# A fused attention and feed-forward kernel: shorter k transposes, a moved fill mark, a split last tile, and more zero matmuls at the start

## The chip, the cores and the metric

The kernel runs on one core of a Trainium2 chip. A core has a matrix engine (TensorE, "PE" in the profile; its weight loads are listed as "PEld"), a vector engine (VectorE, "DVE"), a scalar engine (ScalarE, "ACT"), a general engine (GpSimd, "POOL") and SyncE ("SP"), which here only issues transfers. Transfers are carried by 16 DMA engines that all queues share. The metric is the device time of one execution in microseconds (us); several runs are made, and their median is used.

## The reference

Attention over 8 batches and 8 heads, with 16 extra "beacon" keys and values put ahead of the 576 ordinary ones, and causal masking of the ordinary ones. The output, 4608 rows of 512, goes through a multiplicative feed-forward network:

```python
k_all = np.concatenate([beacon_k, k], axis=2)      # 16 + 576 keys per head, head size 64
v_all = np.concatenate([beacon_v, v], axis=2)
scores = 1/sqrt(64) * q @ k_all^T, masked, softmax
x = (softmax @ v_all) as (4608, 512)
out = (((x @ w1) * (x @ w2)) @ w3) @ w_out         # w1, w2: 512 x 1024; w3: 1024 x 1024; w_out: 1024 x 512
```

Inputs and output are float32.

## The kernel before

Arithmetic is in 16-bit floats with 32-bit accumulation. w3 and w_out are multiplied into one matrix `Wt` (1024 x 512) first, so that the network needs two products per 512 rows of x: `ff_ab` (x times w1 and w2, their product in `gT`) and `ff_out` (`gT` times `Wt`). The 4608 rows make nine chunks, numbered 0 to 8. A chunk is 96 units, and a unit is one 512-column matmul: 64 units of `ff_ab`, 32 of `ff_out` (four output tiles, `mt` 0 to 3, of eight matmuls each).

Attention goes in 64 steps, eight per batch: for each of four pairs of heads an even and an odd step. `scores(s)` makes the score groups of a step (two groups each; the last group of an odd step is ten matmuls with 80 query columns, which need all five key tiles), `exps` their exponentials on ACT, `mask` the masking on DVE, `values(s)` the products with v and the normalization into `x16`.

There are three stages.

1. Up to step 15 (batches 0 and 1) the instructions stand in an order written out by hand, `ORDER` (L40). Each word is one small piece: `cR` and `cW` cast parts of w3 and w_out, `W` transposes a row tile of w3 on TensorE (L341), `w` evacuates it, `M` multiplies two 128-row pieces into an accumulator of `Wt` (L357, "fuse"), `o` reorders loaded q or k (L185), `T` transposes it on TensorE, `S`, `E`, `K`, `V`, `N` are scores, exponentials, masks, value sums and normalizations. `Z.3` is three matmuls with zeros (L239, 432 columns each); ten of them come ahead of the whole order. `G` puts the later loads on POOL's queue.
2. From step 16 on a loop (L678) emits for each step the next step's scores, this step's values and, between them, `fill[s]` units of the feed-forward network. `fill` comes from `marks` (L532): pairs of a step and the number of units that are to be out when this step begins, with even spacing in between. Units count from 40 at step 16; chunk n begins at unit 32 + 96 (n - 1), so chunk 4 at 320.
3. After step 63 what is left of the network follows without a break (L702).

q, k and v of each batch are loaded by POOL in 128-row chunks, cast on the way (L128, L137, L141 for the beacons). For batches 2 to 7, q and k are then transposed by DMA from SP's queue: `transpose_qk` (L149) for chunks 0 to 4, five of q and five of k. The last q chunk has 64 rows. The last k chunk has 80 (576 + 16 - 512), but its transpose takes all 128; the 48 pad rows of `k16s` were set to zero at the start (L317), and the columns that they would fill in `kTs` too (L249). Batches 0 and 1 are transposed on TensorE instead. Two sets of buffers alternate between batches. When the last pair of heads of a batch is normalized, five DMA transposes on SP bring `x16` into `xT` (L520). So SP's queue is, in order: the q and k transposes of a batch, the x transposes of the batch before, those of the next batch, and so on. POOL's queue holds, in the order of emission, the loads of v for the next batch, of q and k for the batch after that, and the stores of output tiles (L413) of all chunks but the last two; those of the last two go on SP's. At most eight of a queue's transfers are outstanding at a time: the next waits for the eighth before it to land.

## Time and profile before

| | |
|---|---|
| median of 5 runs | 301.95 us (301.19 to 302.72) |
| the profiled execution | 301.76 us |
| its span, first to last instruction | 299.7 us |
| PE, PEld, DVE, ACT, POOL busy, share of the span | 96%, 50%, 55%, 53%, 44% |
| 512-column matmul of `ff_ab` and `ff_out`, x864 | 379 ns each, from issue to end; back to back one each 0.216 us |
| copy of 512 columns from the accumulator, ACT L379 and DVE L411 | 597 and 692 ns |
| DMA transposes of q and k, issue to landing, median | 8.9 us |

How to read it: the span is cut into 40 slices of 7.5 us; a digit is the busy share of an engine in a slice, in tenths. "PEclk" is the clock that was granted to TensorE. A row of stretches (they are given with their start and end) lists for each engine how long it was busy and, in brackets, with how many instructions, then the granted clock, the DMA share and GB/s. A timeline row is start, duration, engine, line, operation, output and input, and in square brackets the idle time before it and what ended that. A row of waits is who waited for whom: us in total, times, longest. A row of the chain of waits is start, duration, and what was done or waited for.

### The profile page before, as it was taken

How to read it: one execution, taken by the hardware profiler on the slowest of the kernel's cores; microseconds unless marked ns; L12 is line 12 of the kernel's file. 1: busy time of each engine (PE TensorE's matmuls, PEld its weight loads, DVE VectorE, ACT ScalarE, POOL GpSimd, SP SyncE). 2: the span in 40 equal slices, each digit the busy share in tenths (PEclk: the TensorE clock that was granted, in tenths of full speed). 3: DMA queues.
4: the chain of work that ended last, by engine and by line, in shares of the span. 5: the costliest groups of instructions: out<-in, count | busy, mean ns of one | idle time of the engine just before them, and what ended most of it. 6: DMA issues, size and time to landing. Idle time of an engine off the chain costs nothing.

```text
span 299.7 us, 6953 instructions
## 1 busy us (share of the span) xinstructions
PE 287.4 (96%) x2801; PEld 150.3 (50%) x2801; DVE 164.1 (55%) x386; ACT 160.3 (53%) x226; POOL 131.4 (44%) x183
## 2 busy tenths in 40 slices
PE   6698999999999999999999999999999999999994
PEld 2445766564455555545554555455555544444441
DVE  3337867774556665465555555555556554344342
ACT  3638868672587756645663667466644650320310
POOL 5679968844756735462565327735311002000000
PEclk9599999999999999999999999999999999999999
DMA  7999999999999999999999999999991015103003
GB/s 255 351 165 180 154 184 190 149 131 130 153 221 143 141 128 164 128 155 187 151 141 127 139 211 115 155 139 247 144 236 72 0 35 148 42 0 140 0 31 112
DMA packets 160256, 42.67 MB, mean 142 GB/s; under 512 B 152288, under 2 KB 155872, under 8 KB 160224
## 3 DMA queue, kind: packets, MB, share of 16 engines
q0 software_dynamic: 112032, 24.91, 97.8%
q1 hardware_dynamic: 48192, 17.31, 40.5%
q8 instruction: 22, 0.36, 0.5%
q14 instruction: 10, 0.08, 0.1%
HBM read 39.32 MB, written 9.44 MB: 163 GB/s over the span
## 4 chain that ended last, share of the span: by engine, by line
PE 74%; DMA 15%; issue 2%; POOL 2%; SPq 2%; DVE 2%; ACT 1%; POOLq 0%; DVEq 0%
PE pm L367 32%; PE pm L401 17%; PE pv L491 9%; PE ps L448 8%; DMA qT<-q 5%; DMA k<-in_k_dram 5%; DMA kT<-k 3%; PE ps L357 3%; PE pm L357 3%; DMA gT<-in_moe_w_dram 2%; PE pm L341 1%; POOL q L128 1%; PE pm L217 1%; POOL k L137 1%; SPq L153 1%
## 5 line engine op out<-in xcount | busy, mean ns | idle before, releaser
L367 PE MATMUL pm<-xT,w 128*128 128x512 f16 x576 | 133.1, 379 | 0.0
L463 ACT ACTIVATE pT<-ps 128x736 f16<-128x736 f32 (+3 forms) x128 | 104.9, 864 | 51.7 <-PE ps L448 48.7
L367 PEld LDWEIGHTS <-w 128*128 128x128 f16 x576 | 53.0, 98 | 57.5 <-issue 0.4
L379 ACT ACTIVATE a_sb<-pm 128x512 f32<-128x512 f32 x70 | 41.8, 597 | 60.4 <-PE pm L367 59.6
L381 DVE TENSOR_TENSOR gT<-pm,a_sb 128x512 f16<-128x512 f32 x72 | 49.6, 690 | 37.9 <-PE pm L367 35.2
L401 PE MATMUL pm<-Wt,gT 128*128 128x512 f16 x288 | 65.6, 379 | 0.4 <-DVE gT L381 0.4
L137 POOL DMA_DIRECT2D va<-in_v_dram x40 | 34.0, 858 | 23.4 <-DMA k<-in_k_dram 11.4
L401 PEld LDWEIGHTS <-gT 128*128 128x128 f16 x288 | 27.2, 98 | 31.1 <-issue 0.5
L491 PE MATMUL pv<-va,pT 128*128 128x65 f16 x960 | 40.8, 194 | 0.7 <-DVE pT L475 0.7
L491 PEld LDWEIGHTS <-pT 128*128 128x128 f16 x960 | 33.7, 97 | 10.6 <-issue 5.2
L413 POOL DMA_DIRECT2D out_dram<-ot x28 | 15.5, 556 | 52.8 <-DVE ot L411 36.7
L411 DVE TENSOR_SCALAR ot<-pm 128x512 f32<-128x512 f32 x36 | 24.9, 691 | 24.9 <-PE pm L401 24.8
L508 DVE RECIPROCAL rd<-pv 128x4 f32<-128x4 f32 x64 | 12.1, 189 | 47.7 <-PE pv L491 47.5
L448 PE MATMUL ps<-qT,kT 64*128 64x80 f16 (+3 forms) x704 | 35.1, 228 | 1.7 <-ACT Wt L591 0.7
L128 POOL DMA_DIRECT2D q<-in_q_dram x35 | 30.0, 858 | 13.5 <-DMA va<-in_v_dram 6.3
L137 POOL DMA_DIRECT2D k<-in_k_dram x35 | 29.7, 848 | 11.5 <-DMA va<-in_v_dram 9.4
L448 PEld LDWEIGHTS <-kT 64*128 64x128 f16 x704 | 20.6, 95 | 26.9 <-issue 23.9
L509 DVE TENSOR_TENSOR x<-pv,rd 128x256 f16<-128x256 f32 x64 | 31.4, 491 | 2.4
L475 DVE TENSOR_TENSOR pT<-pT,MB 128x512 f16<-128x512 f16 (+1 forms) x64 | 20.4, 325 | 0.5 <-ACT pT L463 0.2
L475 DVE TENSOR_TENSOR pT<-pT,MA 128x480 f16<-128x480 f16 x32 | 12.8, 399 | 0.4 <-ACT pT L463 0.4
L341 PE MATMUL pm<-ident,xT 128*128 128x128 f16 x64 | 6.3, 260 | 3.6 <-DVE q L170 3.6
L357 PE MATMUL ps<-wo,wT 128*128 128x512 f16 x32 | 9.2, 438 | 0.0
(70 smaller groups left out, 111.6 us busy)
## 6 DMA issues: line engine op xcount, KB each, us to landing
out_dram<-ot POOLq DMA_DIRECT2D x28, 256.0 KB, 8.9
q<-in_q_dram POOLq DMA_DIRECT2D x28, 128.0 KB, 9.9
va<-in_v_dram POOLq DMA_DIRECT2D x24, 128.0 KB, 9.3
k<-in_k_dram POOLq DMA_DIRECT2D x21, 128.0 KB, 9.9
w<-in_moe_w_dram POOLq DMA_DIRECT2D x4, 512.0 KB, 8.7
out_dram<-ot SPq DMA_DIRECT2D x8, 256.0 KB, 2.0
gT<-in_moe_w_dram SPq DMA_DIRECT2D x3, 512.0 KB, 5.9
gT<-in_moe_w_out_dram SPq DMA_DIRECT2D x2, 512.0 KB, 6.1
```

The costliest lines, as they stand in the source:

```text
L128: nc.gpsimd.dma_start(q16s[b % NB2][:rows, c, :].rearrange("s (h d) -> s h d", h=H), q[b, :, ds(c * P, rows), :].rearrange("h s d -> s h d"),)
L137: nc.gpsimd.dma_start(dst[ds(p0, rows)], src[b, :, ds(s0, rows), :].rearrange("h s d -> s h d"))
L357: nc.tensor.matmul(acc, wT[:, rt, :], wo16[:, rt, :], start=(rt == 0), stop=(rt == NFT - 1),)
L367: nc.tensor.matmul(pm, w12[:, kt, ds(i * DF + kf * P, P)], xT[:, kt, ds(mc * 512, 512)], start=(kt == 0), stop=(kt == NKT - 1),)
L379: nc.scalar.activation(a_sb, pm, AF.Copy, scale=GS)
L381: nc.vector.tensor_tensor(gT[:, kf, :], pm, a_sb, ALU.mult)
L401: nc.tensor.matmul(pm, gT[:, kf, ts(mt, P)], Wt[:, kf, :], start=(kf == 0), stop=(kf == NFT - 1),)
L448: nc.tensor.matmul(ps[:, hh, ds(col, n)], kT[ds(hh * 64, 64), t, ts(jt, P)], qT[ds(hh * 64, 64), t, ds(q0, n)],)
L463: nc.scalar.activation(pT[:, :, ds(GO[g], GW[g])], pss[s, j][:, :, 0 : GW[g]], AF.Exp, scale=scale)
L475: nc.vector.tensor_tensor(blk, blk, m.unsqueeze(1).to_broadcast([P, 2, n]), ALU.mult)
L491: nc.tensor.matmul(pv[:, 2 * n + hh, 0:65], pT[:, hh, ds(col, P)], va[:, jt, 2 * t + hh, 0:65], start=(jn == 0), stop=(jn == len(BLK[i]) - 1),
L509: nc.vector.tensor_tensor(x16[:, ds(tiles[0], ni), ds(t * P, P)].rearrange("p i (h d) -> p i h d", h=2), pv[:, 0 : 2 * ni, 0:64].rearrange ...
```

## The change

Four places, the arithmetic being the same:

- `ORDER`: `Z.3` becomes `Z.7`, four more matmuls with zeros ahead of `W.3`, the second w3 tile to be transposed.
- `transpose_qk`: the last chunk of k is transposed with its 80 rows instead of 128.
- `ff_out`: the last output tile (chunk 8, `mt` 3) is computed, evacuated and stored in two halves of 256 columns. The first is evacuated by DVE, the second by ACT. All other tiles are as before.
- `marks`: a point (43, 320) comes in between (32, 200) and (58, 516). Before, the straight line between these two passed 320 units within step 41.

```diff
 ORDER = """
-cW.0.0.A cR.1.D cW.0.1.A cR.3.D cR.0.A W.1 w.1.A G cR.2.D Z.3 W.3 w.3.A cW.1.1.A W.0
+cW.0.0.A cR.1.D cW.0.1.A cR.3.D cR.0.A W.1 w.1.A G cR.2.D Z.7 W.3 w.3.A cW.1.1.A W.0
...
         rows = min(P, S - c * P)
         nc.sync.dma_start_transpose(qTs[i][:, :, ds(c * P, rows)], q16s[i][:rows, c, :])
-        nc.sync.dma_start_transpose(kTs[i][:, :, ds(c * P, P)], k16s[i][:, c, :])
+        rows = min(P, S + Nb - c * P)
+        nc.sync.dma_start_transpose(kTs[i][:, :, ds(c * P, rows)], k16s[i][:rows, c, :])
...
     def ff_out(mc, gT):
         for mt in range(4):
...
+            last = (mc, mt) == (M // 512 - 1, 3)
+            n = DM // 2 if last else DM
             ot = op.tile([P, DM], FP32, name="ot")
-            nc.vector.tensor_scalar(ot, pm, float(1.0 / GS), None, ALU.mult)
-            queue = nc.gpsimd if mc < M // 512 - 2 else nc.sync
-            queue.dma_start(out[ds(mc * 512 + mt * P, P), :], ot)
+            for c in range(0, DM, n):
+                pm = psM.tile([P, 512], FP32, name="pm")
+                for kf in range(NFT):
+                    nc.tensor.matmul(
+                        pm[:, 0:n],
+                        gT[:, kf, ts(mt, P)],
+                        Wt[:, kf, ds(c, n)],
...
+                if c:
+                    nc.scalar.activation(
+                        ot[:, ds(c, n)], pm[:, 0:n], AF.Copy, scale=float(1.0 / GS)
+                    )
+                else:
+                    nc.vector.tensor_scalar(
+                        ot[:, 0:n], pm[:, 0:n], float(1.0 / GS), None, ALU.mult
+                    )
+                queue = nc.gpsimd if mc < M // 512 - 2 else nc.sync
+                queue.dma_start(out[ds(mc * 512 + mt * P, P), ds(c, n)], ot[:, ds(c, n)])
             yield
...
-    marks = [(2 * NSB, 40), (28, 128), (4 * NSB, 200), (58, 516), (NS, 588)]
+    marks = [(2 * NSB, 40), (28, 128), (4 * NSB, 200), (43, 320), (58, 516), (NS, 588)]
```

## The prediction

> **What bounds the kernel now.** I read the page first, then the waits of TensorE, then the chain, then its timeline around each wait.

> ```profile
> span 299.7 us, 6953 instructions
> PE 287.4 (96%) x2801; PEld 150.3 (50%) x2801; DVE 164.1 (55%) x386; ACT 160.3 (53%) x226; POOL 131.4 (44%) x183
> PE   6698999999999999999999999999999999999994
> DMA  7999999999999999999999999999991015103003
> ```

> TensorE is busy for 287.4 of 299.7 us, so only 12.3 us are idle: 1.27 at the start, 3.58 in the first wait for w3, about 4.4 behind the last matmul, and 3 in small pieces. The DMA row is full until slice 29 (about 220 us). Two resources are saturated at once, and an edit pays only where it helps both.

> ```profile
> PE pm L341 <- DVE q L170: 3.6, 1, 3.6
> PE ps L448 <- DMA kT<-k: 0.3, 1, 0.3
> ```

> The waits name both edits' places. The first (the releaser is really the cast of w3 that ends 0.06 us earlier, at 9.76) is where the zero matmuls go. The second is small in time, but the chain shows what it means:

> ```profile
> 181.43 9.19 DMA kT<-k
> 190.62 0.05 issue
> 190.67 0.35 PE ps L448 x10
> ```

> The ten matmuls at 190.67 are the last score group of step 49, which needs the transposed chunk 4 of k of batch 6. They begin 0.05 us after it lands. In step 41 (batch 5) the same group waited 0.34 us, until 161.27, for a landing at 161.22; in step 25 (batch 3) it ran at 101.25 with the landing at 101.04. I call these landings the gates; batches 4 and 7 have 2.2 and 1.3 us of slack. Between gates TensorE has no idle time, so the feed-forward fill just covers what the DMA takes per batch.

> **Zero matmuls, Z.3 to Z.7.** Timeline and stretches:

> ```profile
> 5.53 0.71 PE L242 MATMUL pv<-zeros 128*128 128x432 f16 x3
> 9.82 1.89 PE L341 MATMUL pm<-ident,xT 128*128 128x128 f16 x16 [3.58 <-DVE q L170]
> 5.33:8.74 3.41, 0.91 (x9) 0.40 (x6) 0.00 (x0) 2.23 (x4) 0.00 (x0) 1.00 0.96 376
> 8.74:12.15 3.41, 2.33 (x18) 1.98 (x19) 1.79 (x4) 2.12 (x3) 2.06 (x3) 0.50 1.03 419
> 12.15:15.56 3.41, 3.41 (x15) 1.74 (x14) 1.35 (x4) 2.32 (x4) 3.35 (x7) 0.50 1.19 227
> ```

> Four more at 0.71/3 = 0.24 us, or 0.18 back to back, end near 7.0 instead of 6.24, and at half clock (0.38 each, as the first ten) still before 9.82: they cost nothing, covered by the 3.58 us. The wait stays; what can change is the clock. It fell to 0.50 at 8.74 and returned at 15.56, so 9.82 to 15.56 ran at half speed: 5.74 us of work that needs 2.87. Will it hold? The row: a stretch of 3.41 us with 0.91 busy (27%) was followed by the fall; with four more it has about 1.65 (48%). The stretch from 20 to 24 us, with TensorE busy for 2.79 of 4.00 us (70%), kept it. [...] I give it 55%.

> If it holds, I follow the written order at full speed: two groups of eight transposes at 0.46 us, the ACT copy of wT (1.01 us), two fuses per M word at 0.43. The first q transposes then stand at 15.65, 0.03 after the q copy that waits for its DMA (15.26 + 0.36), instead of 18.26: 2.6 us. Behind it the order c.1, c.0, ok.1 keeps about 2.4. The ends: 0 and 2.9.

> **Pad rows.** Each k chunk 4 of batches 2 to 7 moves 80 rows instead of 128. In the packet records 576 transposed rows make 2304 packets of 256 bytes, so 48 rows are 192 of 512 packets. SP's issue doesn't shorten: chunks of 64 and 128 rows both take about 1.25 us. Counting packets in the order of issue, those of chunk 4 of batches 3, 5 and 6 ran for 2.35, 2.14 and 1.51 us; 37.5% of these is 0.88, 0.80 and 0.57 earlier. I take these: a backlog is there, so a shorter transfer ends sooner. Earlier batches' cuts relieve the shared queues by 192 x 0.02 us / 16 = 0.25 each (0.02 us a packet in the quiet stretch at 243 us). With nothing queued it would be worth 0; if all cuts add up in full, about 0.9 each.

> **Chunk 4 at step 43.** From step 32 to 42 fill falls from 12.15 to 10.9 matmuls a step, from 43 to 57 it is 13.07. The sum of work is the same. But ahead of step 41's group there are 287 units instead of 297, ahead of step 49's 385 instead of 394: TensorE arrives 10 x 0.216 = 2.16 us and 9 x 0.216 = 1.94 us earlier at gates where it has no slack, and what it waits there is not made up, since the fill is only moved behind them. Queued behind a group that waits are the value sums of the step before, its normalization, and all of the step's fill; for them wait the x transposes on SP. The evacuations that go with the moved units (ACT 0.60, DVE 0.69 us each) move along, on engines that are busy for 53 and 55% and have room. It also has the queues' orders move a little: on POOL one output tile of chunk 3 goes behind the v(6), q(7), k(7) loads and one of chunk 4 behind v(7), 0.73 us of DMA each, behind no gate that is tight; on SP the order stays, but the x transposes of batch 4 are issued up to 2 us earlier and with them the queue behind. What it can buy: chunk 4 begins at 168.03, 1.46 us after its last x tile lands at 166.57. That wait doesn't exist before, so the gain is 0 here.

> **Last rows in halves.** 16 matmuls of 256 columns stand for 8 of 512: the same columns, 1.73 us. Weight loads (98 ns) fit under 109 ns. The final evacuation was

> ```profile
> 295.27 0.69 DVE L411 TENSOR_SCALAR ot<-pm 128x512 f32<-128x512 f32 x1 [1.03 <-PE pm L401]
> ```

> and is now an ACT one of 256 columns: 512 take 597 ns, 1024 take 1022, so about 0.39. That saves 0.30. The last DMA carries half (2.0 us from issue to landing before): 0 to 0.2. SP's two issues are 0.33 us each, and the first half's lies under the second half's matmuls. Tail: -0.4.

> **The sum,** against the profiled execution (301.76 us with a span of 299.7; the median of 301.95 is 0.2 above). Clock held. At batch 3 TensorE comes 2.4 early, but the gate moves only 0.88 + 0.25, plus its slack of 0.21: 1.3 passes. Gate 5: 161.22 - 0.80 - 3 x 0.25 - 0.8 = 158.9, where the 0.8 is most of the 1.3 by which SP's x transposes of batch 3 (waiting for TensorE at 128.45) and the queue behind them start earlier. Behind gate 5 lie 299.7 - 161.27 = 138.4 us plus the 2.16 moved there, less the tail 0.4: end at 299.1. Gate 6: 190.62 - 0.57 - 4 x 0.25 - 0.5 (x transposes of batch 4 issued earlier) = 188.55; plus 109.03 + 1.94 - 0.4: 299.1. Both agree: -0.6 of span, so 301.3 for the median. (Without gates it would be the floor of the third rival below.)

> **Rivals.**
> *The clock falls anyway* (27%). Then gate 5 moves by 1.55 only, to 159.7: 299.9, or 0.2 above before, and the median is 302.1. [...]
> *The gates don't move* (22%): slower. The place is step 41's last group. If landing stays at 161.22, the end is 161.22 + 138.4 + 2.16 - 0.4 = 301.4: +1.7, a median of 303.6. It decides where gate 5 gains less than 0.8 (+0.3%), that is, little more than nothing. For it: landings follow each other by about 1.3 us for 64 and 128 rows alike, as if SP's issue set the pace. Against: 1336 packets stood ahead of chunk 4 at 152.43, a backlog that a shorter transfer shortens.
> *The DMA follows TensorE all the way* (11%): all waits go, -2.4 - 0.3 - 0.4 = -3.1, 298.8. For it: SP's starts in batches 4 to 6 wait for TensorE. Against: POOL waits for a landing at nearly every load, whatever TensorE does.
> My own case has 40%, with a range of 300.0 to 302.3.

> **How the numbers follow.** A measurement of this kernel tells some 0.3% (0.9 us) from no change: 301.05 to 302.85. Of my 40%, 20 are below and 20 within; of the clock rival's 27, 5 below, 17 within and 5 above; of the gates', 3 within and 19 above; the last's 11 all below. That makes 36, 40 and 24. My case's gains are cut twice by gates whose shortening I count packet by packet, at the low end of what a backlog may give; for that 4 go from within to below. The range leaves out the far half of the last two: 299.1 to 303.3.

> **What would show it.** Clock: granted 1.00 from 9.8 to 15.5 and the first q transposes near 15.7; else 0.50 again. Pads: chunk 4's issue to landing near 8 us instead of 8.8 and 9.2. Fill: waits of ps for kT in steps 25, 41 and 49, of about 1 us each; if there is none, the gates moved further than I say. Tail: an ACT evacuation of about 0.39. Wrong if x or v landings become the waits, or if the clock falls in some later idle piece.

## The result, and the profile after

The changed kernel's median is 300.76 us (43 runs, 297.24 to 308.29), against 302.49 us for the kernel before, run beside it (80 runs, 299.41 to 310.43). Its time is 0.9945 of the time before, with an interval of 0.9926 to 0.9964: about 0.55% faster. The forecast was 301.3 us with a range of 299.1 to 303.3. Executions of one kernel spread by up to 3.7% here, and the ratios leave out those more than 1.5% above the fastest of their kernel; a ratio and the quotient of two medians can therefore differ by up to 0.7%, so both are given where they do.

The profiled execution took 300.28 us with a span of 298.4. Four lines of the page answer to those shown of before:

```profile
span 298.4 us, 6983 instructions
PE 286.2 (96%) x2813; PEld 150.2 (50%) x2813; DVE 164.2 (55%) x386; ACT 161.0 (54%) x227; POOL 130.8 (44%) x183
PE   7789999999999899999999999999989999999994
DMA  7999999999999999999999999999981014103003
```

TensorE is still idle for 12.2 us (298.4 - 286.2), nearly the 12.3 of before. What fell is its busy time, by 1.2 us, although twelve matmul instructions more were run: at a granted clock of 1.000 in the mean, against 0.987, the same work took less time. The timeline of TensorE at the place of the zero matmuls:

```profile
6.12 1.46 PE L243 MATMUL pv<-zeros 128*128 128x432 f16 x7
9.51 1.07 PE L342 MATMUL pm<-ident,xT 128*128 128x128 f16 x16 [1.93 <-DVE q L171]
10.41 0.59 PE L358 MATMUL ps<-wo,wT 128*128 128x512 f16 x2
10.84 0.61 PE L342 MATMUL pm<-ident,xT 128*128 128x128 f16 x8
11.29 4.05 PE L358 MATMUL ps<-wo,wT 128*128 128x512 f16 x18
15.60 0.43 PE L197 MATMUL pm<-ident,o 96*128 96x96 f16 x6 [0.26 <-DVE o L186]
```

And its stretches, cut in steps of 3.41 us from 6.14, where the record of its full clock begins (start and end, sum, busy time and instructions of PE, PEld, DVE, ACT and POOL, then the granted clock):

```profile
6.14:9.55 3.41, 1.48 (x10) 0.63 (x9) 0.69 (x2) 2.45 (x3) 0.00 (x0) 1.00 1.02 410
9.55:12.97 3.42, 3.42 (x34) 2.24 (x35) 2.12 (x4) 2.68 (x4) 3.19 (x5) 1.00 1.01 376
```

After a stretch with 1.48 of 3.41 us busy (43%) the clock stayed at 1.00, where in the kernel before it fell to 0.50 after 0.91 (27%). The sixteen transposes take 1.07 us instead of 1.89, and the first q transposes start at 15.60 (forecast: 15.65; before: 18.26). Step 16 begins at 75.18 instead of 77.94.

So 2.76 us were gained by step 16, and the span is shorter by only 1.3. Most of the rest was given back in waits. TensorE waited twice for a DMA transpose, for 2.0 us in all, at the last score groups of step 25 and of step 57:

```profile
99.41 0.35 PE L460 MATMUL ps<-qT,kT 64*128 64x80 f16 x10 [0.76 <-DMA kT<-k]
218.70 0.35 PE L460 MATMUL ps<-qT,kT 64*128 64x80 f16 x10 [1.27 <-DMA kT<-k]
```

The second is also in the chain that ended last; it is the last transfer that TensorE waited for in the whole execution:

```profile
208.37 10.29 DMA kT<-k
218.66 0.04 issue
218.70 0.35 PE ps L460 x10
```

The gates, landing of chunk 4 of k / start of the score group that needs it:

| batch (step) | before | after |
|---|---|---|
| 3 (25) | 101.04 / 101.25 | 99.37 / 99.41, waited 0.76 |
| 4 (33) | 129.44 / 131.59 | 126.19 / 129.76 |
| 5 (41) | 161.22 / 161.27 | 156.79 / 156.95 |
| 6 (49) | 190.62 / 190.67 | 183.74 / 186.42 |
| 7 (57) | 218.54 / 219.85 | 218.66 / 218.70, waited 1.27 |

Gates 5 and 6 came 4.4 and 6.9 us earlier, gate 7 not at all. Its transfer was the slow one: issued at 208.37, it took 10.3 us to land, while chunk 4 of batches 3, 5 and 6 took 7.8, 7.7 and 7.6 (before: 8.1, 8.8 and 9.2).

The tail ends as forecast, with the second half's evacuation on ACT:

```profile
293.71 0.42 DVE L421 TENSOR_SCALAR ot<-pm 128x256 f32<-128x256 f32 x1 [0.18 <-PE pm L407]
294.59 0.38 ACT L417 ACTIVATE ot<-pm 128x256 f32<-128x256 f32 x1 [7.19 <-PE pm L407]
```

### The profile page after: what moved, and what is told of

Its sections match the earlier page's. It is cut to its first block, busy times and chain, and to the rows that moved or that the text cites. A ratio compares the mean times of both kernels' runs of the same rounds, so it can differ in the third digit from the quotient of the medians.

```text
span 298.4 us, 6983 instructions
## 1 busy us (share of the span) xinstructions
PE 286.2 (96%) x2813; PEld 150.2 (50%) x2813; DVE 164.2 (55%) x386; ACT 161.0 (54%) x227; POOL 130.8 (44%) x183
## 4 chain that ended last, share of the span: by engine, by line
PE 42%; DMA 35%; POOL 9%; issue 8%; DVE 1%; SPq 1%; ACT 1%; POOLq 0%; DVEq 0%
DMA k<-in_k_dram 20%; PE pm L368 19%; PE pm L407 10%; DMA kT<-k 6%; POOL q L128 4%; PE pv L503 4%; PE ps L460 3%; POOL k L137 3%; DMA va<-in_beacon_v_dram 3%; PE pm L358 3%; DMA gT<-in_moe_w_dram 2%; DMA va<-in_v_dram 2%; DMA q<-in_q_dram 2%; POOL va L137 1%; PE pm L218 1%
## 5 line engine op out<-in xcount | busy, mean ns | idle before, releaser
L407 PE MATMUL pm<-Wt,gT 128*128 128x512 f16 (+1 forms) x296 | 65.9, 373 | 0.4 <-DVE gT L382 0.4
L407 PEld LDWEIGHTS <-gT 128*128 128x128 f16 x296 | 27.9, 98 | 30.1 <-issue 0.5
L503 PEld LDWEIGHTS <-pT 128*128 128x128 f16 x960 | 33.9, 97 | 10.9 <-issue 5.0
L425 POOL DMA_DIRECT2D out_dram<-ot x28 | 15.5, 556 | 54.2 <-DVE ot L421 39.7
L421 DVE TENSOR_SCALAR ot<-pm 128x512 f32<-128x512 f32 (+1 forms) x36 | 24.6, 684 | 23.8 <-PE pm L407 23.7
L128 POOL DMA_DIRECT2D q<-in_q_dram x35 | 30.0, 858 | 10.4 <-DMA va<-in_v_dram 5.3
L358 PE MATMUL pm<-wo,wT 128*128 128x512 f16 x32 | 8.8, 380 | 0.0
L358 PEld LDWEIGHTS <-wT 128*128 128x128 f16 x64 | 5.3, 97 | 4.8 <-issue 0.6
```

What stands on the lines that cost most here:

```text
L128: nc.gpsimd.dma_start(q16s[b % NB2][:rows, c, :].rearrange("s (h d) -> s h d", h=H), q[b, :, ds(c * P, rows), :].rearrange("h s d -> s h d"),)
L407: nc.tensor.matmul(pm[:, 0:n], gT[:, kf, ts(mt, P)], Wt[:, kf, ds(c, n)], start=(kf == 0), stop=(kf == NFT - 1),)
L421: nc.vector.tensor_scalar(ot[:, 0:n], pm[:, 0:n], float(1.0 / GS), None, ALU.mult)
L503: nc.tensor.matmul(pv[:, 2 * n + hh, 0:65], pT[:, hh, ds(col, P)], va[:, jt, 2 * t + hh, 0:65], start=(jn == 0), stop=(jn == len(BLK[i]) - 1),
```

## The experiments

Twelve kernels were run, in three groups with the kernel before beside each. The table gives the ratio to before with its interval, the medians, and in how many executions the clock held throughout (mean granted clock 0.997 or more; one half-speed window of 3.41 us gave 0.994 in e1's profile, two gave 0.987 in that of before). The 44 executions of the changed kernel are its 43 runs and the profiled one. The median of before is 302.6 and 302.7 us in the first two groups and 304.11 in the third, so ratios of the third group look better than medians across groups.

| run | ratio to before | median / before's | clock held |
|---|---|---|---|
| changed kernel | 0.9945 (0.9926 to 0.9964) | 300.76 / 302.49 | 21 of 44 |
| e1_z3 | 0.9965 (0.9939 to 0.9991) | 301.20 / 302.59 | 0 of 22 |
| e2_pads | 0.9993 (0.9959 to 1.0028) | 300.91 / 302.59 | 9 of 14 |
| e3_marks | 0.9922 (0.9886 to 0.9957) | 299.26 / 302.59 | 6 of 9 |
| e4_whole | 0.9964 (0.9938 to 0.9991) | 301.21 / 302.59 | 12 of 22 |
| s1_z7 | 0.9977 (0.9915 to 1.0038) | 302.66 / 302.72 | 5 of 14 |
| s2_nopads | 1.0036 (1.0002 to 1.0070) | 301.73 / 302.72 | 1 of 22 |
| s3_mark43 | 1.0080 (1.0039 to 1.0122) | 304.05 / 302.72 | 0 of 22 |
| e5_z12 | 0.9965 (0.9925 to 1.0005) | 299.85 / 302.72 | 13 of 22 |
| f1_nov | 0.9837 (0.9787 to 0.9887) | 298.77 / 304.11 | 4 of 6 |
| f2_nov_marks | 0.9817 (0.9771 to 0.9864) | 298.31 / 304.11 | 4 of 6 |
| f3_nov_before | 0.9890 (0.9847 to 0.9932) | 300.76 / 304.11 | 0 of 6 |
| g1_fill | 0.9839 (0.9781 to 0.9897) | 298.42 / 304.11 | 6 of 6 |

### One part undone at a time

**The zero matmuls back to three.**

```diff
-... cR.2.D Z.7 W.3 w.3.A ...
+... cR.2.D Z.3 W.3 w.3.A ...
```

> The changed kernel with three zero matmuls again; the rest of the change stays. My account: the clock falls to 0.50 in the first wait and returns near 15.5 us, step 16 begins about 2.4 us later than in the changed kernel, and of that some 1.1 to 1.3 us are taken up by the waits for kT (1.1 in step 25, 1.3 in step 57 of the changed kernel's profile), so the time goes up by 0.8 to 1.3 us: ratio to the kernel before about 0.998. Rival, the early gain is paid out in full: up by 2.4, ratio 1.002. Rival, the DMA gates swallow it: unchanged, ratio 0.9945.

The clock fell in all 22 executions. Two stretches of the profiled one show the window before the fall and the window at half speed:

```profile
6.36:9.77 3.41, 0.62 (x4) 0.14 (x3) 0.69 (x2) 2.23 (x3) 0.00 (x0) 1.00 1.01 402
9.77:13.18 3.41, 3.41 (x27) 2.86 (x28) 2.08 (x4) 1.53 (x2) 3.17 (x5) 0.50 1.05 377
```

One half-speed window costs, by estimate, half of its 3.41 us, 1.7. Yet the kernel is only 0.2% (0.6 us by ratio, 0.4 by median) slower than the changed one, and the two intervals overlap. Step 16 began at 76.86, 1.7 later, but the profile has one wait of 0.7 us in place of two of 2.0 in all:

```profile
PE ps L460 <- DMA qT<-q: 0.7, 1, 0.7
```

In these two profiles the later TensorE waits less, as it would if part of what the clock gives is taken back at the gates; but one profile each does not show it, for the next run held its clock and waited for 0.7 us too. Over all executions the mean granted clock is 0.9959 in the changed kernel and 0.9906 here; over 300 us the difference is 1.6 us at full speed (an estimate), of which 0.4 to 0.6 arrive in the time. Within the changed kernel's own executions, those with the clock held have a median of 300.28 us, those with half-speed windows (0.991 to 0.994) 301.42, a difference of 1.1 us; without the executions that the ratios leave out it is 0.35 (300.11 and 300.46). Either is less than 2.4.

**All 128 rows of the k chunks again.**

```diff
-        rows = min(P, S + Nb - c * P)
-        nc.sync.dma_start_transpose(kTs[i][:, :, ds(c * P, rows)], k16s[i][:rows, c, :])
+        nc.sync.dma_start_transpose(kTs[i][:, :, ds(c * P, P)], k16s[i][:, c, :])
```

> The changed kernel with all 128 rows in the last k transpose again. My account: the last k chunk's packets take about 0.8 us longer and the gates of batches 3, 5, 6 and 7 are 0.8 to 1.5 us later, so the waits for kT grow and the time goes up by 0.8 to 1.5 us: ratio about 0.998. Rival, landings are paced by SP's issue of 1.25 us whatever the rows: unchanged, 0.9945.

By ratio this is 0.5% slower than the changed kernel, so that nearly the whole gain is gone; by medians it is 0.05% slower. Nine of 14 executions held the clock. The wait for kT was 0.7 us, in step 25:

```profile
PE ps L459 <- DMA kT<-k: 0.7, 1, 0.7
```

Gate 7 landed at 216.58, ahead of the changed kernel's 218.66, with the longer transfer. One execution's landings cannot price the pads.

**The old marks.**

```diff
-    marks = [..., (4 * NSB, 200), (43, 320), (58, 516), (NS, 588)]
+    marks = [..., (4 * NSB, 200), (58, 516), (NS, 588)]
```

> The changed kernel with the old marks (no point at step 43). By my prediction's sum the mark costs 2 us at the gates of steps 41 and 49, so without it the kernel is faster by 1 to 2 us: ratio about 0.989. Rival: in the changed kernel's profile those gates have 0.2 and 2.7 us of slack, so the mark costs nothing: ratio 0.9945. Second rival: without it chunk 4 waits for its x tiles (landing 162.3 us in the changed kernel's profile) and the kernel is slower by 0.5 to 1.5 us.

The fastest of this group: 0.9922, a median of 299.26. TensorE's waits have no line for kT or qT in its profile. Without the mark the change would have gained 0.8% (ratio) to 1.1% (medians) instead of 0.55%. The intervals of this run and of the changed kernel overlap, so it does not show the mark's cost alone; the next group does.

**The last tile whole.**

```diff
-            last = (mc, mt) == (M // 512 - 1, 3)
+            last = False
```

> The changed kernel with the last output tile in one piece. My account: one evacuation of 0.69 us on DVE in place of 0.38 on ACT and a 256 KB store at the end: slower by 0.3 to 0.4 us, ratio about 0.9957. Rival, the end is set by the landing of any store and the two halves gain nothing: 0.9945.

0.2% slower than the changed kernel, with intervals that overlap. The tail of its profile, to be read against the ACT row of 0.38 above:

```profile
295.51 0.69 DVE L421 TENSOR_SCALAR ot<-pm 128x512 f32<-128x512 f32 x1 [1.03 <-PE pm L407]
```

The evacuation is 0.31 us longer, and the store behind it takes 2.01 us from issue to landing instead of 1.73 for the half. Together 0.59 us, 0.2%: the measured times agree with the trace, but are too uncertain to show it by themselves.

### One part alone

```diff
# s1_z7: before, with
-... cR.2.D Z.3 W.3 w.3.A ...
+... cR.2.D Z.7 W.3 w.3.A ...
# s2_nopads: before, with
-        nc.sync.dma_start_transpose(kTs[i][:, :, ds(c * P, P)], k16s[i][:, c, :])
+        rows = min(P, S + Nb - c * P)
+        nc.sync.dma_start_transpose(kTs[i][:, :, ds(c * P, rows)], k16s[i][:rows, c, :])
# s3_mark43: before, with
+    marks = [..., (43, 320), ...]
```

> The kernel before with seven zero matmuls and nothing else. The runs so far list a granted clock: with three zeros nearly every execution has 0.986 to 0.994 (one or two windows of 3.4 us at half speed), with seven about half have 0.997 to 1.000. My account: the clock is held in about half of the executions, and of the 2.4 us that this is worth at step 16 the gate of step 25 (slack 0.21 us, k chunk 4 with 128 rows) takes most: 0.2 to 0.6 us in the median, ratio 0.998 to 0.9995. Rival, no gate: half of 2.4 us, 1.2 us, ratio 0.996.

Nothing that can be told from no change: 0.9977 with an interval of more than half a per cent to each side, and equal medians. Five of 14 executions held the clock. The profiled execution, the fastest of the 14, held it, with a span of 295.5 us and no wait for kT or qT; the median shows no such gain.

> The kernel before with 80 rows in the last k transpose and nothing else. My account: in the kernel before TensorE waits only 0.3 us for kT, so alone this is worth 0.3 to 0.6 us: ratio 0.998 to 0.999. Rival, the kT waits of a typical execution are larger than in the profiled one, and the cut is worth by itself what taking it out of the changed kernel cost (0.48%): ratio 0.995.

Inconclusive. The ratio says 0.4% slower, the medians of all executions say 0.3% faster. The effect of the pads alone is below what this measurement can tell.

> The kernel before with the point (43, 320) in the marks and nothing else. My prediction's term: TensorE comes 2 us earlier to gates without slack and waits there: slower by 1.5 to 2 us, ratio 1.005 to 1.0065. Sized by what taking the mark out of the changed kernel gave (0.23%): 1.002. Rival, the mark costs nothing: 1.000 with no more wait for kT than before.

Slower by 0.8% (0.4 to 1.2); by medians 0.4%. This is the one part with a cost of its own that an interval keeps clearly away from zero. Some of it may be the clock of the first 25 us, which the mark does not touch: the mean granted clock over all executions is 0.9880 against 0.9892, an estimated 0.4 us of 300. The profiled execution waited at a transfer, though at another than chunk 4 of k, in step 48:

```profile
185.40 0.39 PE L448 MATMUL ps<-qT,kT 64*128 64x256 f16 x4 [1.27 <-DMA qT<-q]
```

Over all profiles with v loaded, TensorE's waits for kT and qT sum to 2.0 us in the changed kernel, 0.7, 0.7, 2.1 and 1.3 in the others with the mark at 43 (e1, e2, e4, s3), a mean of 1.4; with the old marks to 0.3, 0, 0, 0, 0 and 0.7 (before, e3, s1, s2, e5, g1), a mean of 0.2. But some of these waits are in steps 24 and 25, ahead of step 32, from which on the marks differ: 0.76 us in the changed kernel, 0.67 in e2, 1.16 in e4, 0.7 in g1. Without them the means are 0.84 and 0.06. The difference, 0.8 us, is at the low end of what the mark costs by the two measures in the two pairs: 0.23 to 0.8%, 0.7 to 2.4 us. The waits account for a part of the cost, perhaps not for all.

This execution lost the clock in a second window as well, from 23.30 to 26.71:

```profile
19.88:23.30 3.42, 2.21 (x33) 1.56 (x33) 2.58 (x6) 1.82 (x3) 1.60 (x3) 1.00 2.11 165
23.30:26.71 3.41, 3.41 (x27) 1.79 (x26) 2.72 (x6) 1.91 (x3) 3.26 (x5) 0.50 1.73 185
```

### More zeros, and the second place where the clock falls

```diff
-... cR.2.D Z.7 W.3 w.3.A ...
+... cR.2.D Z.12 W.3 w.3.A ...
-    marks = [..., (43, 320), ...]
```

> The changed kernel with the old marks and twelve zero matmuls in place of seven (they end near 8.4 us at full clock and 9.7 at half clock, and the cast of w3 that the next transposes wait for is done near 9.5). If the clock follows how much of the wait is filled, nearly every execution has a mean granted clock of 0.997 or more and the kernel is faster than the same with seven zeros by what the unheld half loses, 0.3 to 0.6 us: ratio 0.990. Rival, the clock's phase decides whatever the number of zeros: half of the executions stay at 0.994 and the ratio is that of seven zeros, 0.992.

What was expected did not come: five zeros more held the clock in 13 of 22 executions, hardly more often than seven did (21 of 44 in the changed kernel, 27 of 45 in e2, e3 and e4), with a median of 299.85 (299.15 for the 13), and the kernel is not faster than e3. The profiled execution shows one way in which it is lost: the clock held in the first wait and fell at 23.06. Its stretches, and TensorE's timeline in the first of them:

```profile
19.65:23.06 3.41, 2.20 (x34) 1.64 (x34) 2.58 (x6) 1.89 (x3) 2.44 (x4) 1.00 1.75 174
23.06:26.47 3.41, 3.38 (x26) 1.67 (x22) 2.46 (x6) 1.84 (x3) 2.63 (x4) 0.50 2.09 173
```

```profile
20.33 0.33 PE L460 MATMUL ps<-qT,kT 64*128 64x128 f16 x4 [0.54 <-DVE Wt L603]
20.59 0.43 PE L197 MATMUL pm<-ident,o 96*128 96x96 f16 x6
20.96 0.18 PE L199 MATMUL pm<-ident,b 16*128 16x16 f16 x1
21.81 0.39 PE L460 MATMUL ps<-qT,kT 64*128 64x256 f16 x4 [0.67 <-ACT Wt L603]
22.13 0.62 PE L342 MATMUL pm<-ident,xT 128*128 128x128 f16 x8
22.59 0.42 PE L197 MATMUL pm<-ident,o 96*128 96x96 f16 x6
```

TensorE was busy for 2.20 of 3.41 us (64%), with no gap over 0.67 us, and lost its clock all the same; at 43% it was held in the changed kernel. What differs is what ran. L197, L199 and L342 are transposes. The table counts the busy time of a stretch for the products alone (scores, fuses, zeros), with the clock that followed:

| window | all busy | products alone | clock after it |
|---|---|---|---|
| s2, 7.65 to 11.06 | 1.06 (31%) | 0.15 (4%) | fell |
| f3, 6.97 to 10.39 | 0.88 (26%) | 0.28 (8%) | fell |
| e1, 6.36 to 9.77 | 0.62 (18%) | 0.59 (17%) | fell |
| e2, 8.60 to 12.02 | 1.78 (52%) | 0.59 (17%) | held |
| s3, 6.23 to 9.64 | 0.99 (29%) | 0.66 (19%) | fell |
| before, 5.33 to 8.74 | 0.91 (27%) | 0.71 (21%) | fell |
| e5, 19.65 to 23.06 | 2.20 (64%) | 0.98 (29%) | fell |
| s1, 18.03 to 21.44 | 2.20 (64%) | 0.99 (29%) | held |
| s3, 19.88 to 23.30 | 2.21 (65%) | 1.00 (29%) | fell |
| f1, 6.61 to 10.02 | 1.75 (51%) | 1.19 (35%) | held |
| changed, 19.79 to 23.20 | 2.61 (77%) | 1.26 (37%) | held |
| changed, 6.14 to 9.55 | 1.48 (43%) | 1.44 (42%) | held |

(In these profiles the changes of clock of one execution are whole multiples of 3.41 us apart: 3.41, 6.83 and 283.31 us in the kernel before, which is 1, 2 and 83 steps; edges of windows in which nothing fell are counted on in such steps from the execution's change of clock at its end.) By all busy time the windows do not sort: 65% fell and 43% held. By products they nearly do. In the fourteen profiles, the seven windows that a fall followed are all in the table, with 29% or less, and of the windows at full clock that none followed, some 1,100, only e2's and s1's have as little as 29%. Near 29% both happen. e2's window is a plain exception, and its cause is open; TensorE was idle for 3.05 us in and before it, and 3.95 us passed without a product:

```profile
8.60:12.02 3.42, 1.78 (x26) 1.51 (x27) 1.94 (x4) 2.42 (x3) 1.51 (x2) 1.00 1.02 412
```

That the transposes are the cause was not shown: no run changes them alone. The longest gap does not sort the windows either: e5 lost its clock with no gap over 0.67 us, or 1.15 between products, and the changed kernel held it through a gap of 1.93 up to 9.51, or 2.83 between products up to 10.41.

### Fewer transfers

Three kernels leave out the loads of v for batches 3 to 7, so that DMA has less to carry: the changed kernel (f1), the changed kernel with the old marks (f2), and the kernel before (f3).

```diff
-            for c in range(NJT):
-                load_v(b + 1, c)
```

> The changed kernel without the loads of v for batches 3 to 7 (their value sums use what lies in the buffers; all of TensorE's, ACT's and DVE's work stays). That takes 30 of some 110 loads from the POOL queue in the loop. If the mark costs time by the waits for kT and qT at the gates, these waits are gone here: no wait for kT or qT over 0.3 us in all, and the same time within 0.15% as the next kernel, which has the old marks: about 298 us, ratio 0.985. Rival, the mark costs by something on TensorE or its evacuations: 0.4% slower than the next kernel.

> As the kernel before it, with the old marks (no loads of v for batches 3 to 7). Gates as the cause: the same as with the point at step 43, ratio 0.985. Rival: 0.4% faster than it.

> The kernel before without the loads of v for batches 3 to 7. With no gate left, what separates it from the changed kernel without these loads is the clock (two windows at half speed are worth up to 2.9 us, one 1.7; held in about half of the executions with seven zeros) and the tail of 0.35 us: 1.4 to 2.0 us slower than the two above, about 300 us, ratio 0.991. Rival, the change gains mainly by the DMA transposes' pad rows: then no more than the tail separates them.

Each is faster than its full version, and the six executions of each spread little: 297.74 to 299.89, 297.28 to 299.50, and 299.78 to 301.07. In the kernel before, fewer transfers took off 1.1% (0.989). f1 and f2 are 0.15% apart by medians (298.77 and 298.31) and 0.2% by ratio: with room on the queues the mark seems to cost little, as it should if it costs through late landings. Their intervals of 0.5% to each side do not by themselves exclude the 0.4% of the rival. f2 also missed what was expected of it, for it still waited 1.3 us for kT, though in step 25, ahead of the steps in which the marks differ. f1's waits have no line for kT or qT; f2's have this one:

```profile
PE ps L460 <- DMA kT<-k: 1.3, 1, 1.3
```

f3 is 2.0 us slower than f1. With the gates eased, the clock, the halves, the pads and the mark together give the changed kernel 2.0 us, where with all transfers they gave 1.7 by medians. The profiled f3 shows the clock's share, a window lost after one with 0.88 us busy:

```profile
6.97:10.39 3.42, 0.88 (x13) 0.61 (x12) 0.77 (x3) 1.96 (x2) 0.33 (x1) 1.00 1.03 412
10.39:13.80 3.41, 3.41 (x22) 2.18 (x20) 2.07 (x4) 2.52 (x3) 3.41 (x6) 0.50 1.07 335
```

### A version that is faster than both

In e5 and s3 the clock fell at a second place. The last kernel has the old marks, twelve zeros at the first place, and three and four more between the transposes from 18.8 us on:

```diff
-... cR.2.D Z.7 W.3 w.3.A ...
+... cR.2.D Z.12 W.3 w.3.A ...
-... ok.1 S.0.0 c.2.D c.3.A Tk.1 ek.1.D S.0.1 W.4
+... ok.1 Z.3 S.0.0 c.2.D c.3.A Tk.1 ek.1.D Z.4 S.0.1 W.4
-    marks = [..., (43, 320), ...]
```

> The changed kernel with the old marks, twelve zero matmuls in the first wait, three more ahead of the first score group and four ahead of the second, where TensorE is idle for 0.54 and 0.67 us near 20 and 21.5 us. In the run with twelve zeros alone the clock fell once more at 23.06, behind a window with little but transposes in these idle pieces. If that is why a third of its executions stay at 0.994, nearly all are at 0.997 or more here and the ratio is 0.988. Rival: the zeros delay what follows and the clock falls elsewhere, ratio 0.991 or more.

The clock held in all six executions. The time is 0.9839 of before (0.9781 to 0.9897), a median of 298.42; the interval lies below that of the changed kernel, with which it was not run side by side. Its old marks may be part of that: by medians it is 0.8% faster than the changed kernel, but only 0.3% faster than e3, which has these marks and seven zeros. Six executions are few, and one of them took 302.12 us with its clock held, so the clock is not all that varies. The added zeros in TensorE's timeline, and the stretch that they fill:

```profile
18.80 0.71 PE L243 MATMUL pv<-zeros 128*128 128x432 f16 x3
20.23 0.90 PE L243 MATMUL pv<-zeros 128*128 128x432 f16 x4
```

```profile
19.00:23.70 4.70, 4.66 (x60) 2.82 (x59) 3.78 (x9) 3.30 (x5) 2.90 (x6) 1.00 1.90 168
```

TensorE was idle for 0.04 us there. In e5 it had waited 1.2 us for evacuations, ahead of the score groups at 20.33 and 21.81; the zeros took the place of those waits.

## Why the prediction was right, and where it was not

**Zero matmuls: right, with a chance where there is a share.** In the profiled execution the clock stayed up, the first q transposes came within 0.05 us of the forecast, and 2.76 us were gained by step 16 (forecast 2.4). Over all executions the clock held in 21 of 44 (48%), so "the clock falls" was not an alternative but the other half of them; the 55%, the author's estimate and not worked out from a run, was near this share. The sign of being wrong that was named last, a fall in some later idle piece, came true in e5 and s3. Where the changed kernel's other executions lose their clock is not shown: none of the seven profiles with seven zeros has a fall before the end. The falls in the first wait, in the kernels with three zeros, came anywhere from 8.74 to 11.06 us, at another time in each profile; that this decides which executions hold the clock was not shown.

**"The gate moves only 0.88 + 0.25": the idea held, the sizes did not.** A gain ahead of the gates arrives in part only: of some 1.6 us of clock 0.4 to 0.6 came out when it was undone (e1), and nothing that can be told when it was made alone (s1, within 0.6%). But gates 5 and 6 moved by 4.4 and 6.9 us in the profile, where the packet count gave 2.3 and 2.1. So the waits forecast for steps 41 and 49 were not there. Step 25's was forecast at about 1 us and was 0.76. That the pads caused the larger moves is not shown: e2, with all rows, had gate 5 at 157.85 and gate 6 at 185.58, and s2, with the pads cut but the old clock, 156.46 and 187.56. The landings differ by several us from one kernel's profile to another's (gate 7, with all loads, from 208.9 to 220.6 us), and the packets' count explains less than that.

**The mark: its sign right, its place wrong.** It costs time: 0.8% alone, 0.2 to 0.5% inside the change, 0.7 to 2.4 us against the 2.16 and 1.94 of the prediction. But at steps 41 and 49, where the prediction put the cost, the changed kernel did not wait; it waited at step 57. There the mark itself brings TensorE only 2 units earlier (489 instead of 491 ahead of the group, 0.43 us). The group was reached 2.4 us earlier than before (217.43 instead of 219.85), 2.0 of it from the start (2.76 less the wait of 0.76 in step 25). This used up the 1.3 us of slack, while the transfer did not land earlier.

The step that failed is "behind no gate that is tight", said of the output tile of chunk 4 that the mark moves behind the loads of v(7). In the profiles of all five kernels with the mark and all loads, POOL issues three stores right behind these loads; in the six with the old marks it issues two (before: at 211.28). In the changed kernel they are:

```profile
204.82 1.14 POOL L425 DMA_DIRECT2D out_dram<-ot  x2
206.70 0.54 POOL L425 DMA_DIRECT2D out_dram<-ot  x1 [0.74 <-DMA va<-in_v_dram]
```

In the changed kernel, e2, e4 and s3 all their packets, 192 of 4 KB, ran between the issue and the landing of chunk 4 of k of batch 7, and that transfer took 8.5 to 10.4 us. With the old marks 10 to 128 such packets did, and it took 4.0 to 8.0 us. The fifth kernel with the mark, e1, had 75 of them and 6.9 us; without the v loads (f1 to f3) there were none, and it took 2.3 to 2.4. So the extra store is a likely cause of the late gate 7. It is not shown: a transfer that takes longer also meets more packets, and no run moved that store alone.

**The halves: right, a little small.** 0.59 us instead of 0.4; the estimate of 0.39 for the ACT copy was measured as 0.38, and the smaller store gave 0.28, above the end of 0 to 0.2 that was set for it.

**The sum.** Forecast -0.6 us of span, measured -1.3 in the profile, and -0.55% (about 1.7 us) over all executions. The case named likeliest, clock held and gates following in part, is the one that the profiled execution shows; it was sized too low there because the gates followed further. That the median, 300.76, came out only 0.5 us below the forecast is in part luck: the gates gave more than was counted, and the clock, counted as held, was held in half of the executions. The rival that ended slower, gates that do not move, fell with the landings of gates 3 to 6; it happened at gate 7 alone. "The DMA follows all the way" (298.8) is refuted by the 2.0 us of waits, but e3, which is the change without the mark, had no such wait in its profile and came to 299.26.

**What stays open.** How much the pads are worth, and by what path: the two measures disagree in s2 and in e2. Where the executions of the changed kernel with a lower clock lose it, and why e2's window kept it. And why a transfer of the same size lands several us earlier or later from one profile to the next (gate 6, with 80 rows: 183.74 us in the changed kernel, 187.56 in s2).

## What to carry to other kernels

Where DMA and the matrix engine are both full, as in this kernel, a gain on the engine counts only as far as the landings behind it have slack (of 2.76 us by step 16, 1.3 were left in the span), and moving work away from ahead of a tight landing can cost what was moved (0.7 to 2.4 us for 2.16 and 1.94 moved). Look at every later landing's slack for the sum of all gains, not only at those that are tight now, and ask which stores the moved work puts alongside it. To hold the clock through a thin stretch, count the products in it apart from the transposes (here the seven stretches that lost it had products for 4 to 29% of 3.41 us, and of those that kept it only two had as little), and look for the next thin stretch before filling the first. Where executions spread by more than the effect, look at how often the clock held besides the median.
